# One double bank for the first transforms through the whole first half, full-row modal matmuls and later gating

## The chip, the core and the metric

The kernel runs on one core of a Trainium2 chip. TensorE (PE) multiplies matrices into PSUM, which has 8 banks of 128 x 512 words of 32 bits. VectorE (DVE), ScalarE (ACT) and GpSimd (POOL) do elementwise work, and DVE also transposes blocks of 32 x 32. SyncE (SP) issues nearly all transfers. Each engine works through its own instructions in order. The metric is the device time of one execution in microseconds (us), as the median of several.

## What is computed

Four layers are applied to one sequence of 2048 positions and 512 channels: A, B, A, B, each on a layer norm of x and added to x. Both layers are long causal convolutions per channel, done through Fourier transforms of length 4096.

```python
def _A_ref(q, k, v, shift_k, ssm_k, ssm_D):
    k_shift = 0
    for t in range(ks):
        k_shift = k_shift + k_pad[:, t:t + S, :] * shift_k[:, ks - 1 - t][None, None, :]
    kv = k_shift * v
    y = irfft(rfft(kv_pad) * rfft(kf_pad))[:S]
    y = y + kv * ssm_D[None, None, :]
    return q * y

def _B_ref(u, log_A_real, A_imag, C_real, C_imag, log_dt, D_skip):
    A = -jnp.exp(log_A_real) + 1j * A_imag
    C = (C_real + 1j * C_imag) * dt[:, None]
    P = jnp.exp((A * dt[:, None])[:, :, None] * pos[None, None, :])
    K = 2.0 * jnp.einsum("dn,dnl->dl", C, P).real
    y = irfft(rfft(u) * rfft(K))[:L]
    return y + u * D_skip[None, None, :]

x = x + _A_ref(_layernorm(x), ...)
x = x + _B_ref(_layernorm(x), ...)
x = x + _A_ref(_layernorm(x), ...)
x = x + _B_ref(_layernorm(x), ...)
```

The long convolution inside layer A does not depend on x (it works on `k` and `v` alone), so the kernel computes it once and uses it in both A layers. Layer B depends on x and is convolved twice. Its taps K, a sum over 128 modes for each channel and position, are computed once.

## The kernel before

**Transforms.** A forward transform has two matmul stages. The first stage (`fwd_group` and `fwd_rows`, line 171) multiplies a group of 32 channels by the table `wz`, once for each half `a` of the positions, into a tile `pf`. DVE then transposes `pf` into the tile z (lines 189 and 191; z is called `x`, `zk` or `zu` in the profile by whose it is). The second stage (`f2_chunk`, line 196) makes a tile `pu` with four matmuls. A transform of one quarter of the channels has 4 groups and then 8 chunks `pu`.

The first stage exists in two forms. Where the dictionary `psum` has a key `f1`, the group goes into one double bank (2 banks, 64 of the array's rows for each half, 512 columns). Where it has not, the table's rows of the other half are zero, all 128 rows are used, and the group takes two single banks under the tag `c1` (four matmuls of 256 columns). In the profile each matmul of 32-bit floats is two records, so a group is 4 records `64*128 64x512` in the first form and 8 records `128*128 128x256` in the second.

**Stages.** The first half of the program runs two streams of Python generators side by side, which a scheduler then merges and orders for each engine:

- `diagonal`, for layer A: the spectrum of `ssm_k` by quarters (`spectrum_quarter`, copies to `pc`, written to `spec`); the gating products kv of 16 groups (`gated`: four POOL products `term` on line 629, one ACT copy to a PSUM tile `acc`, three additions and a product `un` on DVE, written to `kv_d`); then `convolution`. A step of the convolution makes a chunk `pu`, multiplies it by the spectrum (ACT lines 281 and 282, DVE line 283, POOL lines 285 and 286, result `vv`), transforms back into `pi` (line 295, copied by ACT on line 296), and for each group through DVE (line 310) into `po` (line 316), which ACT copies to `ya`.
- `stream`, for layer B's taps: 64 steps, each with the angles `pa` (line 494, and line 499 after a rounding on DVE), the magnitudes `pm` (line 479), sines and exponentials on ACT, products `xye` on POOL and DVE, and a contraction into `pk` (line 531). Every four steps give 32 channels of taps, which go out to `kdram` and come back as `kk` for the spectrum of K (tile `zk`).

After both, `gated_update` adds layer A to x, row by row, the statistics and the norm follow, and the convolution of layer B begins.

**PSUM.** `pa` and `pm` share 3 banks and `pk` has one (pool `pp`). The other four banks are a stage pool, opened by `stage_banks`. Until the spectrum of `ssm_k` and the gating are through it holds two single banks `c1` and one double bank `f1`; before the convolution of layer A it is closed and opened again with four banks `c1` and none of the tag `f1`. Only after the first 16 steps of the first B convolution does a third pool take all 8 banks, 4 as `c1` and two double banks `f1`.

**Modal rows.** `load_rows` loads the modal parameters of 32 channels into `raw` (two kinds `k` on 128 partitions) and casts them to `rw`. Partitions 0 to 63 belong to steps 0 and 1 of the group and 64 to 127 to steps 2 and 3, so `mags` and `angles` multiply 64 rows at a time.

**Order.** The order of the code gives priorities. `run_steps` takes turns between one step of `stream` and two of `diagonal`. Before, one group of `gated` stands right behind the first step of the spectrum, and one third of a group (`next(kvs, 0)`) behind each of the 48 spectrum steps.

## Time and profile before

| | us |
|---|---|
| median of 3 runs | 742.3 |
| lowest and highest of them | 741.83, 750.0 |
| the profiled execution | 734.99 |
| span of its instructions | 733.2 |

The span is the time from the first to the last instruction of the profiled execution. It stands 1.8 us under that execution's own time, and 9.1 us under the median. Rows of the profile give a start and a duration in us; `x8` says that eight like instructions were merged into the row. A busy time counts a matmul from its start to the modelled end of its results, so that the share of a busy PE in which its array really streams is smaller.

By the profile, the first `pu` of layer A's convolution begins at 208.99 us and its last copy `ya` at 422.4 us. The update of x begins at 431.2 us, and the first `pu` of layer B's convolution at 480.64 us.

### The profile page before, as it was taken

What the parts mean: (1) busy time and instruction counts of PE and PEld (TensorE: products, weight loads), DVE (VectorE), ACT (ScalarE), POOL (GpSimd) and SP (SyncE); (2) the same over time, 40 slices, a digit from 0 to 9 for tenths busy, and PEclk for the clock granted to TensorE, in tenths of its full rate; (3) what the DMA queues carried; (4) which work ended last, traced back from release to release, by engine and by line L of the source; (5) the groups of instructions that cost most, each with busy time, mean ns of one, the idle gap of its engine ahead of it and who ended that gap; (6) DMA issues with size and microseconds to landing.
All of it is one profiled execution on the core that took longest, in us unless ns stands there. A gap on an engine that the chain in (4) does not pass through costs nothing. (4 is left out here: it accounts for less than half of the span.)

```text
span 733.2 us, 14282 instructions
## 1 busy us (share of the span) xinstructions
PE 593.9 (81%) x4984; PEld 409.9 (56%) x4984; DVE 531.1 (72%) x961; ACT 486.0 (66%) x882; POOL 454.8 (62%) x473
## 2 busy tenths in 40 slices
PE   1378877698989999969998865899798817799996
PEld 0154554456766776736765454767476503476773
DVE  7857959877385785584574877376597998978775
ACT  4246566577678777776798749677655447768672
POOL 5847969678268595684596620157576612479693
PEclk9997979768999999989999996999999978899999
DMA  9769767774745457636457493567866360178682
GB/s 324 258 227 315 255 209 235 226 249 158 223 125 143 130 127 204 167 107 173 118 149 212 136 335 150 170 181 203 226 192 164 85 172 0 51 209 238 195 244 100
DMA packets 80683, 135.39 MB, mean 185 GB/s; under 512 B 8540, under 2 KB 29412, under 8 KB 79460
## 3 DMA queue, kind: packets, MB, share of 16 engines
q1 hardware_dynamic: 79716, 132.06, 60.3%
q0 software_dynamic: 896, 2.43, 1.2%
q8 instruction: 39, 0.64, 0.4%
q14 instruction: 32, 0.26, 0.1%
HBM read 98.80 MB, written 35.65 MB: 183 GB/s over the span
## 5 line engine op out<-in xcount | busy, mean ns | idle before, releaser
L285 POOL TENSOR_TENSOR sw<-sw,kab 128x512 f32<-128x512 f32 x96 | 124.9, 1305 | 66.3 <-ACT sw L282 61.3
L283 DVE TENSOR_TENSOR vv<-pu,kab 128x512 f32<-128x512 f32 x96 | 65.1, 680 | 64.1 <-ACT sw L282 44.1
L295 PE MATMUL pi<-vv,mm 128*128 128x128 f32 x768 | 105.7, 281 | 6.7 <-DVE vv L283 4.3
L286 POOL TENSOR_TENSOR vv<-vv,sw 128x512 f32<-128x512 f32 x76 | 98.6, 1301 | 14.5 <-DVE vv L283 12.0
L295 PEld LDWEIGHTS pi<-vv,mm 128*128 128x128 f32 x768 | 94.2, 193 | 20.6 <-issue 10.4
L281 ACT ACTIVATE sw<-pu 64x512 f32<-64x512 f32 x96 | 57.1, 595 | 65.7 <-PE pu L196 61.8
L171 PE MATMUL pf<-kk,wz 128*128 128x256 f32 (+1 forms) x176 | 64.7, 624 | 42.1 <-issue 15.2
L517 POOL TENSOR_TENSOR xye<-co,m 128x512 f32<-128x512 f32 x64 | 76.0, 1187 | 36.5 <-ACT co L507 12.5
L629 POOL TENSOR_TENSOR term<-kvt 128x512 f32<-128x512 f32 x64 | 81.5, 1292 | 19.5 <-ACT acc L635 9.8
L196 PEld LDWEIGHTS pu<-zu,w 128*128 128x128 f32 x512 | 63.0, 191 | 42.8 <-DVE vv L283 16.1
L196 PE MATMUL pu<-x,w 128*128 128x128 f32 x512 | 79.6, 302 | 5.9 <-ACT pc L247 2.5
L196 PEld LDWEIGHTS pu<-x,w 128*128 128x128 f32 x512 | 70.7, 209 | 21.9 <-issue 7.5
L196 PE MATMUL pu<-zu,w 128*128 128x128 f32 x512 | 72.8, 284 | 10.7 <-DVE vv L283 9.6
L171 PE MATMUL pf<-u,wz 128*128 128x256 f32 (+2 forms) x280 | 76.4, 485 | 3.0 <-DVE zu L189 1.2
L247 ACT COPY pc<-pu 128x512 f32<-128x512 f32 x64 | 37.2, 587 | 45.3 <-PE pu L196 22.6
L485 ACT ACTIVATE m<-pm 128x512 f32<-128x512 f32 x96 | 53.4, 607 | 18.5 <-PE pm L479 15.1
L316 PE MATMUL po<-w,w 128*64 128x512 f32 x192 | 53.9, 637 | 13.8 <-DVE w L310 12.0
L171 PEld LDWEIGHTS pf<-kk,wz 128*128 128x128 f32 (+1 forms) x176 | 30.1, 222 | 58.2 <-issue 29.3
L505 ACT ACTIVATE co<-pa 128x512 f32<-128x512 f32 x64 | 38.4, 600 | 30.2 <-PE pa L499 29.8
L282 ACT COPY sw<-pu 64x512 f32<-64x512 f32 x96 | 55.5, 578 | 1.1
L518 DVE TENSOR_TENSOR xye<-pa,m 128x512 f32<-128x512 f32 x64 | 43.7, 683 | 13.8 <-ACT pa L506 7.3
L479 PE MATMUL pm<-tg,rw 64*128 64x512 f32 x96 | 43.7, 517 | 10.5 <-DVE xye L519 8.3
(137 smaller groups left out, 1147.3 us busy)
## 6 DMA issues: line engine op xcount, KB each, us to landing
kab<-spec SPq DMA_DIRECT2D x188, 256.0 KB, 4.3
spec<-pc SPq DMA_DIRECT2D x64, 256.0 KB, 2.3
kvt<-kv_in SPq DMA_DIRECT2D x16, 624.0 KB, 5.3
yaq<-ya_d SPq DMA_DIRECT2D x5, 1024.0 KB, 7.5
kk<-ssmk_in SPq DMA_DIRECT2D x16, 256.0 KB, 5.1
kv_d<-un SPq DMA_DIRECT2D x16, 256.0 KB, 4.1
xt<-x_in SPq DMA_DIRECT2D x16, 256.0 KB, 2.9
kdram<-ks SPq DMA_DIRECT2D x64, 64.0 KB, 2.9
```

The lines of the kernel that those rows point to most:

```text
L171: yield T.matmul(o, w, rhs, start=True, stop=True)
L196: ins = T.matmul(pu[:, i, :], w2[:, c * CK + i, :], z[:, :, c * CK + i, :], start=True, stop=True)
L281: S.mul(sw[0:64], pu[64:128], -1.0)
L282: swapped[0] = S.copy(sw[64:128], pu[0:64])
L283: V.tensor_mul(vv, pu, kabs[s][:, 0])
L285: (V if last else G).tensor_mul(sw, sw, kabs[s][:, 1])
L286: (V if last or s % add_dve == add_dve - 1 else G).tensor_add(vv, vv, sw)
L295: i1s[t] = T.matmul(pi[:, i, :], mm[:, c * CK + i, :], vvs[t][:, i, :], start=True, stop=True)
L316: ins = T.matmul(po[64 * a:64 * a + 64], w4, ws[g][:, :, 16 * a:16 * a + 16, :].rearrange("p x t r -> p t x r"), start=True, stop=True, ti ...
L485: i = S.activation(m, pm.rearrange("p (c i) -> p c i", c=16 if col == 2 else 8), AF.Exp)
L517: G.tensor_mul(xye[:, 0, :, 32:96], co[:, :, 1:65], m[:, :, 32:96])
L629: G.tensor_mul(term, kvt[:, 3 - j:19 - j, :], tap(j))
```

## The change

Five edits go together.

1. The second call `stage_banks(4, 0)` is gone. The stage pool keeps two banks `c1` and the double bank `f1` through layer A's convolution, so that all first stages of the first half take the pair form.
2. The stage pool and the pool of `pa` and `pk` are closed, and the pool of 4 banks `c1` and two double banks is opened, before `gated_update` rather than after the first 16 steps of the B convolution.
3. `raw` and `rw` get one more dimension, h: for each half the 64 other partitions are zero. `mags` and `angles` multiply all 128 rows. Two fixed tiles `raw` are zeroed once, and the tensor `rows_d` becomes one.
4. No group of `gated` stands in front any more (KV0 = 0), and the thirds of groups begin behind the fourth spectrum step (KS = 3).
5. The prologue of layer A's convolution (7 steps of `main`) is merged with the gating that is left over.

```diff
     def load_rows(gi):
-        raw = wk.tile([128, 2, 128], F32, name="raw", tag="raw", bufs=2)
+        raw = raws[gi % 2]
         q, g = divmod(gi, 4)
-        for k in range(2):
-            nc.sync.dma_start(raw[:, k, :], rows_d[k][q, :, g, :])
-        rows[gi] = wk.tile([128, 2, 128], F32R, name="rw", tag="rw", bufs=2)
+        for h in range(2):
+            hs = slice(64 * h, 64 * h + 64)
+            nc.sync.dma_start(raw[hs, h], rows_d[:, q, hs, g, :].rearrange("k p n -> p k n"))
+        rows[gi] = wk.tile([128, 2, 2, 128], F32R, name="rw", tag="rw", bufs=2)
         V.tensor_copy(rows[gi], raw)
...
-        rhs = tabs["tg2"][hs] if col == 2 else tabs["tg1"][hs, 8 * s:8 * s + 8, :]
-        mt = T.matmul(pm, rows[gi][hs, 1, :], rhs, start=True, stop=True)
+        rhs = tabs["tg2"] if col == 2 else tabs["tg1"][:, 8 * s:8 * s + 8, :]
+        T.matmul(pm, rows[gi][:, h, 1, :], rhs, start=True, stop=True)
...
-        T.matmul(pa, rows[gi][hs, 0, :], tabs["tt"][hs, 8 * s:8 * s + 8, :], start=True, stop=False,
+        T.matmul(pa, rows[gi][:, h, 0, :], tabs["tt"][:, 8 * s:8 * s + 8, :], start=True, stop=False,
...
-        KV0 = 1
+        KV0 = 0
+        KS = 3
...
-                    if q == 0 and i == 1:
-                        for grp in range(KV0):
-                            for _ in gated(grp):
-                                pass
...
-                    next(kvs, 0)
+                    if 12 * q + i >= KS:
+                        next(kvs, 0)
...
+            main = convolution(0, {"conv": ap}, steps_a, finish_a, lag=LAGA, ahead=AHA, nk=NKA, ns=NSA, nw=NWA, inplace=True,
+                               add_dve=ADA, zlast=zlast)
+            for _ in range(NCH - 1):
+                next(kvs, 0)
+                next(main)
+                yield
             for _ in kvs:
                 yield
-            stage_banks(4, 0)
-            yield from convolution(0, {"conv": ap}, steps_a, finish_a, lag=LAGA, ahead=AHA, nk=NKA, ns=NSA, nw=NWA, inplace=True,
-                                   add_dve=ADA, zlast=zlast)
+            yield from main
...
+    sctx.close()
+    pctx.close()
+    pp2 = ctx.enter_context(tc.tile_pool(name="ps2", bufs=1, space=PSUM, reuse_waits="tile"))
+    psum["c1"] = (pp2, 4)
+    psum["f1"] = (pp2, 2)
     with ExitStack() as yctx:
         yp = sbuf(yctx, "yp", "right")
...
     gctx.close()
-    sctx.close()
-    pctx.close()
-    pp2 = ctx.enter_context(tc.tile_pool(name="ps2", bufs=1, space=PSUM, reuse_waits="tile"))
-    psum["c1"] = (pp2, 4)
-    psum["f1"] = (pp2, 2)
     pools["conv"] = sbuf(ctx, "conv_b")
```

Three places of the merged order follow. Rows give the line, the operation, the tiles (output, then inputs) and the shape of the access. Lines from 460 on move by a few in the changed kernel: 472 becomes 479, 479 becomes 485, 494 becomes 499, 499 becomes 504, 531 becomes 536.

The first place is DVE at the start of the program, behind the last preparation of the modal parameters. Here `x<-pf` transposes a group of the `ssm_k` spectrum, `acc` and `un` belong to the gating, and `rw` is the cast of the modal rows with which the 64 tap steps begin. Before:

```order
L189 STREAM_TRANSPOSE x<-pf 128x512 x2
L637 TENSOR_TENSOR acc<-acc,term 128x512 x5
L639 TENSOR_TENSOR un<-acc,kvt 128x512
L637 TENSOR_TENSOR acc<-acc,term 128x512
L189 STREAM_TRANSPOSE x<-pf 128x512 x2
L639 TENSOR_TENSOR un<-acc,kvt 128x512
L189 STREAM_TRANSPOSE x<-pf 128x512 x2
L637 TENSOR_TENSOR acc<-acc,term 128x512
L472 CAST rw<-raw 128x256 x2
```

And now:

```order
L189 STREAM_TRANSPOSE x<-pf 128x512 x6
L479 CAST rw<-raw_234 128x512
L479 CAST rw<-raw_237 128x512
L642 TENSOR_TENSOR acc<-acc,term 128x512 x3
L644 TENSOR_TENSOR un<-acc,kvt 128x512
```

Nine gating instructions that stood ahead of the casts stand behind them now, and the casts have twice the columns.

The second place is PE in layer A's convolution, early in its run. Before, with single banks and full rows for `pf`, and half rows for `pa<-tt,rw`:

```order
L295 MATMUL pi<-vv,mm 128x128 x4
L171 MATMUL pf<-u,wz 128x16x8x2 x4
L499 MATMUL pa<-y,minus 128x512
L494 MATMUL pa<-tt,rw 128x512 x2
L171 MATMUL pf<-kk,wz 128x16x8x2 x4
L531 MATMUL pk<-xye_231 32x64 x16
L196 MATMUL pu<-x,w_104 128x128 x4
```

And now:

```order
L171 MATMUL pf<-u,wz 128x16x16x2 x2
L196 MATMUL pu<-x,w_103 128x128 x4
L295 MATMUL pi<-vv,mm 128x128 x3
L536 MATMUL pk<-xye_232 32x64 x16
L485 MATMUL pm<-tg_202,rw 128x512 x2
L295 MATMUL pi<-vv,mm 128x128
L171 MATMUL pf<-u,wz 128x16x16x2 x2
```

A group of the first stage is two matmuls here where it was four, on 64 rows where it was on 128; `pu`, `pi` and `po` now take turns on two banks.

The third place is PE at the end of layer A's convolution, from its last `po` on. Before:

```order
L316 MATMUL po<-w,w_106 64x512 x2
L171 MATMUL pf<-kk,wz 128x16x8x2 x8
L531 MATMUL pk<-xye_231 32x64 x16
L531 MATMUL pk<-xye_233 32x64 x16
L171 MATMUL pf<-kk,wz 128x16x8x2 x4
L196 MATMUL pu<-zk,w_104 128x128 x32
L171 MATMUL pf<-kk,wz 128x16x8x2 x16
L196 MATMUL pu<-zk,w_104 128x128 x32
L171 MATMUL pf<-u,wz 128x16x8x2 x16
L196 MATMUL pu<-zu,w_104 128x128 x4
```

And now:

```order
L295 MATMUL pi<-vv,mm 128x128 x12
L316 MATMUL po<-w,w_105 64x512 x8
L196 MATMUL pu<-zk,w_103 128x128 x32
L171 MATMUL pf<-kk,wz 128x16x16x2 x8
L196 MATMUL pu<-zk,w_103 128x128 x32
L171 MATMUL pf<-u,wz 128x16x16x2 x10
L196 MATMUL pu<-zu,w_103 128x128 x12
```

The last two contractions `pk` and three of the seven groups `pf<-kk` that stood behind the last `po` now stand ahead of it, and five groups of layer B's first stage, not four, stand ahead of its first `pu`. Over the whole program, up to the last `pu<-zk`, PE changes 132 times between 64-row and full 128 x 128 matmuls before and 72 times now.

More of the change, by code (lines that the diff above doesn't have):

```diff
@@ L118 @@
     kv_d = [dram.tile([128, 512], F32, name=f"kv_d{g}") for g in range(16)]
-    rows_d = [dram.tile([NQ, 128, 4, 128], F32, name=f"rows_d{k}") for k in range(2)]
+    rows_d = dram.tile([2, NQ, 128, 4, 128], F32, name="rows_d")
     cpool = sbuf(ctx, "cpool")
@@ L457 @@
         factors.append(xye)
+    raws = []
+    for i in range(2):
+        raw = wk.tile([128, 2, 2, 128], F32, name=f"raw{i}")
+        for h in range(2):
+            G.memset(raw[64 - 64 * h:128 - 64 * h, h], 0.0)
+        raws.append(raw)
     rows, ms, pks, angs = {}, {}, {}, {}
@@ L491, in angles @@
         h, s = divmod(k, 2)
-        hs = slice(64 * h, 64 * h + 64)
         pa = pp.tile([128, 512], F32, name="pa", tag="pa", bufs=NPA)
-        T.matmul(pa, rows[gi][hs, 0, :], tabs["tt"][hs, 8 * s:8 * s + 8, :], start=True, stop=False,
+        T.matmul(pa, rows[gi][:, h, 0, :], tabs["tt"][:, 8 * s:8 * s + 8, :], start=True, stop=False,
                  skip_group_check=True)
```

2 lines of the change are left out of this document (1 added, 1 removed).

## The prediction

> **What bounds the kernel now.** I read the busy times by stage first, then the chain of waits where the two layers meet, then single matmuls in the timeline. Stretches of the span, with the busy time of each engine (number of instructions in brackets), the granted TensorE clock, and the DMA share:
>
> ```profile
> span 733.2 us, 14282 instructions
> core 0: us, PE busy (x) PEld busy (x) DVE busy (x) ACT busy (x) POOL busy (x), PEclk, DMA share, GB/s
> 39.00:209.00 170.00, 142.48 (x1288) 92.85 (x1288) 123.97 (x229) 106.94 (x187) 113.88 (x123) 0.86 0.70 228
> 209.00:423.00 214.00, 193.37 (x2120) 137.63 (x2121) 142.72 (x229) 169.31 (x293) 152.06 (x155) 0.98 0.55 150
> 423.00:481.00 58.00, 39.92 (x277) 33.87 (x276) 35.81 (x86) 40.53 (x89) 7.51 (x16) 0.88 0.66 221
> ```
>
> In the 214 us in which layer A's convolution runs beside the taps, PE is busy 90%, ACT 79%, POOL 71%, DVE 67%. PE is the first limit there and ACT the next. In the 170 us before, PE has 84% and DVE 73%. From 423 to 481 us no engine is full, so a chain of waits sets the time. The chain that ended last shows it (start, us, what):
>
> ```profile
> 423.45 3.63 DMA kk<-kdram
> 428.17 6.91 DMA yaq<-ya_d
> 435.15 7.51 DMA yaq<-ya_d
> 455.90 2.66 DMA kk<-kdram
> 465.39 3.57 DMA spec<-pc
> 472.39 1.99 PE pf L171 x8
> 474.38 5.46 PE pf L171 x24
> 480.64 1.16 PE pu L196 x8
> ```
>
> So the last quarter of the taps (kk) and the update of x (yaq) are woven together there, and layer B's first stage (4 groups, 32 records of pf from 472.39) comes behind both.
>
> **The start (edit 4).** POOL, DVE and PE in the timeline (start, us):
>
> ```profile
> 26.74 8.71 POOL L629 TENSOR_TENSOR term<-kvt 128x512 f32<-128x512 f32 x7 [2.29 <-ACT acc L635]
> 28.13 3.16 DVE L637 TENSOR_TENSOR acc<-acc,term 128x512 f32<-128x512 f32 x5
> 35.41 0.24 POOL L239 TENSOR_TENSOR kk<-kk,dr 1x32 f32<-1x32 f32 x1
> 39.19 3.78 PE L196 MATMUL pu<-x,w 128*128 128x128 f32 x16 [1.41 <-DVE x L189]
> 43.26 2.07 DVE L472 CAST rw<-raw 128x256 fp32r<-128x256 f32 x2
> ```
>
> The fourth group of the spectrum waits at 35.41 for the small POOL addition kk, which stands behind seven products term (8.71 us). By the order now only four products stand ahead of it, so up to 3 x 1.24 = 3.7 us go, and DVE has nine gating instructions (9 x 0.63 = 5.7 us by the row of five) out of the way of the casts rw. The first pu and the first tap step should come 4 to 6 us earlier. The gating is only moved: the three groups that come later (12 POOL products of 1.24 us) fall into stretches in which POOL is 67 to 71% busy, and they are wanted only when their channels are transformed, so I cost them at nothing; without that cover they would cost at most 12 x 1.24 = 15 us of POOL. I take -5 us, between 0 and -6. The casts get twice the columns: at 2.07 / 2 = 1.04 us each, 16 casts that double would add at most 17 us of DVE over the whole first half; DVE is not the limit, so nothing is added.
>
> **Pairs of 64 rows instead of full rows (edits 1 and 2).** PE in the timeline, first full-row work in a row, then pairs between full-row work:
>
> ```profile
> 248.90 1.05 PE L196 MATMUL pu<-x,w 128*128 128x128 f32 x8
> 249.79 1.05 PE L295 MATMUL pi<-vv,mm 128*128 128x128 f32 x8
> 205.09 1.99 PE L171 MATMUL pf<-u,wz 128*128 128x256 f32 x8
> 206.74 0.82 PE L499 MATMUL pa<-y,minus 128*128 128x512 f32 x2
> 481.73 1.13 PE L171 MATMUL pf<-u,wz 64*128 64x512 f32 x4
> 482.79 2.05 PE L196 MATMUL pu<-zu,w 128*128 128x128 f32 x16
> 484.77 1.13 PE L171 MATMUL pf<-u,wz 64*128 64x512 f32 x4
> 485.83 1.16 PE L196 MATMUL pu<-zu,w 128*128 128x128 f32 x8
> ```
>
> A full group keeps PE 206.74 - 205.09 = 1.65 us. A group as pairs keeps it 485.83 - 484.77 = 1.06 us. Eight full records take 249.79 - 248.90 = 0.89 us where no 64-row work is near, but the sixteen from 482.79 take 1.98, not 1.78: 0.20 us for the change of form. So a group saves 1.65 - 1.26 = 0.39 us alone and up to 0.59 where pairs stand together; I take 0.5. Of 32 groups that change form, 16 (layer A) and 5 (zk) lie in the full 214 us: 21 x 0.5 = 10.5 us of PE. The other 7 of zk and 4 of layer B lie in the chain after 423 us; there PE is busy 69% and waits for transfers and copies, so of at most 11 x 0.5 = 5.5 us I count 1 us.
>
> **Full rows for the modal matmuls (edit 3).** In the timeline a half-row pa, its full-row partner and the next half-row one, and then a full-row one before a pu:
>
> ```profile
> 203.82 0.49 PE L494 MATMUL pa<-tt,rw 64*128 64x512 f32 x1
> 204.24 0.49 PE L499 MATMUL pa<-y,minus 128*128 128x512 f32 x1
> 204.67 0.49 PE L494 MATMUL pa<-tt,rw 64*128 64x512 f32 x1
> 258.49 0.71 PE L499 MATMUL pa<-y,minus 128*128 128x512 f32 x2
> 259.03 1.05 PE L196 MATMUL pu<-x,w 128*128 128x128 f32 x8
> ```
>
> With a change of form each takes 0.42 us; without one, two take 259.03 - 258.49 = 0.54 us. A half-row stretch and the way back thus cost 0.85 - 0.54 = 0.31 us. The order counts 132 changes between 64 rows and the full array before and 72 now; the 48 groups of pairs bring nearly all of the 72 and are already priced with theirs, those of before some 30 of the 132. About 100 changes, 50 round trips, go: 50 x 0.31 = 15 us of PE, of which 37 of the 64 tap steps, so 9 us, lie in the full 214 us and 6 in the 170 us before. There PE has slack, and I count half, -3 us. Two half-row matmuls on different halves could have run side by side before; that loss is inside the 0.31, since it was taken from neighbours that don't.
>
> **What the two missing banks cost (edit 1).** One pu in the timeline:
>
> ```profile
> 208.99 2.28 PE L196 MATMUL pu<-x,w 128*128 128x128 f32 x18
> 211.12 0.59 ACT L281 ACTIVATE sw<-pu 64x512 f32<-64x512 f32 x1
> 211.73 0.58 ACT L282 COPY sw<-pu 64x512 f32<-64x512 f32 x1
> 212.34 0.69 DVE L283 TENSOR_TENSOR vv<-pu,kab 128x512 f32<-128x512 f32 x1 [1.63 <-ACT sw L282]
> ```
>
> From its first matmul to the end of vv a bank is held 213.03 - 208.99 = 4.0 us. A pi, po or chunk of zk has one ACT copy of 0.58 us instead of the three readers, so about 2.2 us with its matmuls. The stage has 32 pu, 32 pi, 16 po and 16 chunks of zk: 32 x 4.0 + 64 x 2.2 = 269 us of bank time. Over four banks that is 67 us each and no matter; over two it is 134 us of about 200, so a bank is often still held when PE comes to it. The trace has this very layout, two banks c1 and a double bank, in the 170 us before, where 32 pu and 16 acc use them. Who waited for whom there (total, times, longest):
>
> ```profile
> PEld pu L196 <- ACT pc L247: 4.2, 5, 1.3
> PEld pu L196 <- DVE un L639: 3.7, 5, 1.3
> PE pu L196 <- ACT pc L247: 2.9, 5, 1.1
> ```
>
> That is 7.9 us for 48 uses, 0.16 us a use; 96 uses give 16 us. I take +16. The lower end is half of it (8 us), if the order suits the banks better; the upper end is one ACT instruction of 0.59 us at every use, 57 us. The Trainium skill, TensorEngine Tiling (Array Packing), Gotcha 1 (PSUM Pressure), speaks against the change here: row tiling puts more pressure on PSUM, as different row tiles write to different banks and may not use one at the same time. This case agrees in that a pair takes a double bank out of the four; the page gives no price.
>
> **The end of the stage (edit 2 and the order).** SP issued the second pair of yaq loads late, behind a small load dr that waited for the trip of kk through DRAM (423.45 + 3.63 us, then the yaq of 428.17). The taps now end ahead of the last po, so that wait, about 2 us of the chain, goes. With the 1 us of pairs I count -3 us. The pools' new place costs nothing by itself: the new double banks lie where pa, pm and pk were, which are free by then, and the last chunks of zk only hold the banks that layer B's pu take after them, as before.
>
> **The sum.** Start -5, early stage -3, full stage -10.5 - 9 + 16 = -3.5, end -3: -14.5 us. The profiled execution took 734.99 us and would take about 720.5. The median of the runs is 742.3, 7.3 us over that execution, so the forecast for the median is 742.3 - 14.5 = 728 us, a change of -2.0%, at the edge of what a measurement of this kernel can tell from no change, which I take as 2%, or 14.8 us (727.5).
>
> **The rivals.**
>
> Two banks become the bound. Each of the 96 uses then waits about one ACT instruction, 0.59 us: +57 instead of +16, so 742.3 - 14.5 + 41 = 769 us. For it speaks that ACT is 79% busy and DVE waits for ACT's sw before vv, so a bank comes free late; against it that pu, pi and tap work alternate, and the nearest stretch shows 0.16 us. The change stops paying at (16 + 14.5) / 96 = 0.32 us a use and is slower by 2% from 0.47 us. Chance 0.12.
>
> The banks are covered. PE has the tap matmuls to do while a bank drains; then the 16 us are at most 4, and the time is about 742.3 - 14.5 - 12 = 716 us. For it: taps and layer A are independent, the order was made with two banks in view, and the taps have their own banks. Against it: PE takes its work strictly in order. Chance 0.33.
>
> PE's relief lies beside ACT. If ACT's 169 us with their waits hold the stage, the saved PE time is idle time, and only the start and the end pay: 742.3 - 8 = 734 us. ACT's 79% speaks for it, PE's 90% against. Chance 0.15.
>
> The clock falls. The granted clock is 0.98 where PE is busy 90% and 0.86 where it is 84%. If relief and bank waits bring the full stage to 84%, its PE time of some 170 us grows by 0.12 of itself, 20 us: 748 us. The Trainium skill, TensorE: Matmul & The Clock Gate, Part 1, has the clock drop only after idle windows of about 3.4 us; by that rule waits near 1 us would leave it alone, and the time stays 728. The waits for banks shown above are at most 1.3 us. Chance 0.05.
>
> **How the numbers follow.** The forecast (about 728, both sides of the 2% line) has 0.35, and the rivals 0.33, 0.15, 0.05 and 0.12. Faster by over 2%: the covered banks, 0.33, and somewhat under a third of the forecast's own 0.35, together 0.43. Slower by over 2%: the bound by banks, 0.12. Within 2%: the rest, 0.45. The likeliest case alone reaches from 720 (bank waits of 8 us) to 736. The range leaves out the slower half of the first rival and the far end of the second, where nearly all gains add up: 709 to 750.
>
> **What would show it.** Right: first pu of the spectrum near 35 us and the first cast rw near 35 us; no 64-row records of pm and pa; 4 records of about 0.65 us for every group of pf up to layer A's end; first pu of layer A's convolution some 8 us earlier; waits of PE for ACT sw, ie, pc and DVE vv summing to 10 to 25 us in layer A's convolution, which lasts 205 to 215 us; kk's trip gone from the chain behind the last ya. Wrong: those waits above 45 us, a granted clock under 0.9 in that stage, or a PE that is less busy while the stage keeps its 214 us.

## The result and the profile after

| | before | after |
|---|---|---|
| median of 4 runs each | 742.07 us | 757.12 us |
| lowest and highest | 741.48, 750.0 | 756.28, 766.31 |
| the profiled execution | 734.99 | 766.31 |

The measured ratio is 1.0324, with a 95% interval from 1.0269 to 1.0379. The eight times of the table alone give less, 757.12 / 742.07 = 1.020 by medians; which further times of before the ratio goes by is not known. So the change costs 2 to 3%, 15 to 24 us. The forecast was 728 us with a range of 709 to 750, so sign and range were both missed. The profiled execution of after is the slowest of its four, that of before lies 7 us under its median and under all four: the two traces differ by 31 us, the medians by 15. Differences of less than about 10 us between two traces are therefore not read here unless a second pair of kernels shows them too. Runs of the kernel before on the chips of the experiments lay between 727.95 and 751.32 us, so each experiment is compared with the runs of before on its own chip. In the table of the experiments the ratios leave out runs in a slower state and the medians do not, so the two can differ by about 1% (e15: 737.12 against 741.36 us by medians, ratio 1.0055).

First the same two stretches as were shown of before (busy time of PE, PEld, DVE, ACT and POOL with the number of instructions, then clock, DMA share, GB/s), and the stretch from the first pu of layer A's convolution to its last ya, which the trace of after puts at 221.61 and 449.82 us:

```profile
39.00:209.00 170.00, 135.10 (x1210) 83.61 (x1209) 129.81 (x223) 96.78 (x168) 119.07 (x124) 0.80 0.66 214
209.00:423.00 214.00, 184.29 (x2028) 122.61 (x2026) 144.87 (x237) 170.09 (x296) 150.60 (x157) 0.94 0.55 153
...
222.00:450.00 228.00, 194.08 (x2121) 126.80 (x2121) 146.15 (x234) 167.69 (x292) 155.60 (x159) 0.91 0.53 149
```

Against before, DVE and POOL are busier from 39 to 209 us (129.81 and 119.07 against 123.97 and 113.88 us) while PE is less busy. Layer A's convolution takes 228 us instead of 214. PE's busy time in it did not fall (194.08 against 193.37 us): it has less to stream, but at a clock of 0.91 instead of 0.98, and it idles 34 us instead of 21.

The start, in the timeline of after (start, us, what):

```profile
32.31 3.78 PE L196 MATMUL pu<-x,w 128*128 128x128 f32 x16 [1.41 <-DVE x L189]
35.11 0.67 POOL L464 MEMSET raw<- 64x256 f32 x2 [5.43 <-DMA rows_d<-hl]
38.23 0.43 DVE L479 CAST rw<-raw 128x512 fp32r<-128x512 f32 x1 [5.98 <-DMA raw<-rows_d]
39.48 0.43 DVE L479 CAST rw<-raw 128x512 fp32r<-128x512 f32 x1 [0.82 <-DMA raw<-rows_d]
```

The first pu comes 6.9 us earlier than before (39.19) and the first cast 5.0 us earlier (43.26). Yet the first pu of layer A's convolution comes 12.6 us later (221.61 against 208.99). So the stretch between lost some 18 us and the convolution 14 us.

The forms of the matmuls, in the groups of after up to 510 us (operation, shapes, count, busy us, mean ns, idle us before them and what ended it):

```profile
L485 PE MATMUL pm<-tg,rw 128*128 128x512 f32 x96 | 43.5, 518 | 4.3 <-ACT m L491 3.4 <-DVE rw L479 0.7 <-DVE xye L524 0.2
L499 PE MATMUL pa<-tt,rw 128*128 128x512 f32 x64 | 29.7, 485 | 7.1 <-DVE xye L524 6.1 <-ACT m L491 0.9
L171 PE MATMUL pf<-u,wz 64*128 64x512 f32 x84 | 25.3, 684 | 3.8 <-issue 1.4 <-DVE x L189 1.3 <-DVE zu L189 1.0
```

The change does what it says: pm and pa have all 128 rows, and pf from u stands in pairs of 64 rows only. What PE waited for in after from 222 to 450 us (total, times, longest):

```profile
PE po L316 <- DVE w L310: 7.6, 7, 2.0
PE pu L196 <- ACT x L296: 4.8, 6, 1.3
PE pk L536 <- DVE ks L546: 4.6, 2, 4.3
...
PE pi L295 <- ACT x L296: 2.0, 3, 1.0
PE po L316 <- ACT x L296: 1.6, 2, 0.8
...
PE pu L196 <- DVE vv L283: 1.2, 3, 0.6
```

Waits of pu, pi and po for the ACT copy x of another chunk are waits for a bank. In before the same view, from 209 to 423 us, has one of 0.6 us. Here those quoted, with vv, make 4.8 + 2.0 + 1.6 + 1.2 = 9.6 us. The row pk behind DVE's ks has one wait of 4.3 us; what lies behind it is the main finding below.

The end, in the timeline of after:

```profile
449.23 0.59 ACT L682 COPY ya<-po 128x512 f32<-128x512 f32 x1 [2.82 <-PE po L316]
...
452.08 1.64 SPq L730 DMA_DIRECT2D yaq<-ya_d  x2
...
458.43 1.95 ACT L741 ACTIVATE ut<-yaq,rs 128x512 f32<-128x512 f32 x3 [3.61 <-DMA yaq<-ya_d]
```

From the last ya to the first use of yaq it takes 458.43 - 449.82 = 8.6 us, before 431.2 - 423.0 = 8.2 us. The trip of kk comes behind that, as before:

```profile
461.48 14.40 SPq L248 DMA_DIRECT2D spec<-pc  x5
...
475.97 2.27 SPq L229 DMA_DIRECT2D kk<-kdram  x2
...
478.77 0.24 POOL L239 TENSOR_TENSOR kk<-kk,dr 1x32 f32<-1x32 f32 x1 [44.91 <-DMA kk<-kdram]
...
490.95 6.81 PE L196 MATMUL pu<-zk,w 128*128 128x128 f32 x40 [1.51 <-DVE zk L189]
```

The last taps were done at 429.1 us, but SP issues the last two loads of kk at 475.97, behind five writes of the spectrum (461.48 + 14.40). The spectrum of K waits for them, and layer B's first stage comes behind it. From the last ya to the first pu of layer B (508.3) it takes 58.5 us, before 57.7.

### The profile page after: what moved, and what is told of

Its sections match the earlier page's. It is cut to its first block, busy times and chain, and to the rows that moved or that the text cites. A ratio compares the mean times of both kernels' runs of the same rounds, so it can differ in the third digit from the quotient of the medians.

```text
span 764.5 us, 14021 instructions
## 1 busy us (share of the span) xinstructions
PE 596.0 (78%) x4856; PEld 390.3 (51%) x4856; DVE 535.0 (70%) x961; ACT 485.9 (64%) x882; POOL 455.9 (60%) x477
## 5 line engine op out<-in xcount | busy, mean ns | idle before, releaser
L196 PE MATMUL pu<-x,w 128*128 128x128 f32 x512 | 82.3, 309 | 15.6 <-ACT pc L247 6.9
L196 PEld LDWEIGHTS pu<-x,w 128*128 128x128 f32 x512 | 74.1, 216 | 37.5 <-ACT pc L247 8.9
L171 PE MATMUL pf<-kk,wz 64*128 64x512 f32 x128 | 58.4, 857 | 38.4 <-DMA kk<-ssmk_in 12.6
L196 PE MATMUL pu<-zu,w 128*128 128x128 f32 x512 | 72.7, 285 | 11.2 <-DVE vv L283 10.9
L316 PE MATMUL po<-w,w 128*64 128x512 f32 x192 | 59.8, 712 | 15.4 <-DVE w L310 12.2
L171 PE MATMUL pf<-u,wz 64*128 64x512 f32 (+2 forms) x200 | 61.4, 647 | 5.6 <-DVE zu L189 2.2
L536 PE MATMUL pk<-xye 128*32 128x64 f32 x2048 | 54.3, 244 | 11.2 <-POOL xye L526 6.5
L196 PE MATMUL pu<-zk,w 128*128 128x128 f32 x256 | 42.2, 319 | 22.4 <-ACT pc L247 17.8
L536 PEld LDWEIGHTS pk<-xye 128*32 128x32 f32 x2048 | 39.1, 122 | 39.7 <-issue 20.9
L523 DVE TENSOR_TENSOR xye<-pa,m 128x512 f32<-128x512 f32 x64 | 43.4, 678 | 20.1 <-ACT pa L511 10.9
```

The source lines that it names most:

```text
L171: yield T.matmul(o, w, rhs, start=True, stop=True)
L196: ins = T.matmul(pu[:, i, :], w2[:, c * CK + i, :], z[:, :, c * CK + i, :], start=True, stop=True)
L316: ins = T.matmul(po[64 * a:64 * a + 64], w4, ws[g][:, :, 16 * a:16 * a + 16, :].rearrange("p x t r -> p t x r"), start=True, stop=True, ti ...
L536: T.matmul(pk[32 * i4:32 * i4 + 32, 2 * k + i, :], xye[:, r, 4 * i + i4, 64:96], xye[:, r, 4 * i + i4, 0:64], start=r == 0, stop=r == 1, t ...
```

## The experiments

Each kernel is the kernel before with the edit named, or the changed kernel with a part undone. The edits have the numbers of the section on the change. The table has the median beside that of before on the same chip, the ratio with its interval, and from the trace the first pu of layer A's convolution, its length to the last ya, and the span. For e4 and e8 only the times are given.

| kernel | what it is | median, before (us) | ratio | first pu | length | span |
|---|---|---|---|---|---|---|
| before | | 742.07 | 1 | 209.0 | 214.0 | 733.2 |
| after | edits 1 to 5 | 757.12, 742.07 | 1.0324 [1.0269, 1.0379] | 221.6 | 228.2 | 764.5 |
| e1 | edit 3 | 736.84, 735.75 | 1.006 [1.0013, 1.0106] | 221.1 | 203.2 | 733.6 |
| e2 | edit 4 | 754.70, 735.75 | 1.0288 [1.0216, 1.0361] | 232.9 | 206.9 | 748.1 |
| e3 | edits 1, 2 | 751.78, 735.75 | 1.0256 [1.0193, 1.0320] | 207.8 | 236.8 | 752.1 |
| e4 | edits 2, 3, 4 | 745.97, 735.75 | 1.014 [1.0037, 1.0243] | | | |
| e5 | edits 1, 2, 3, 5 | 753.58, 739.09 | 1.0226 [1.0132, 1.0319] | 209.6 | 230.2 | 749.0 |
| e7 | two single banks | 774.65, 739.09 | 1.0515 [1.0420, 1.0610] | 219.1 | 235.9 | 768.3 |
| e8 | e3, pairs twice | 778.87, 739.09 | 1.0552 [1.0466, 1.0637] | | | |
| e9 | e2, pu twice | 748.42, 739.09 | 1.0165 [1.0067, 1.0264] | 232.5 | 201.3 | 743.3 |
| e10 | three single banks | 750.40, 743.45 | 1.0118 [1.0055, 1.0181] | 212.1 | 221.5 | 748.4 |
| e11 | KV0 = 2 | 753.62, 743.45 | 1.0155 [1.009, 1.022] | 219.9 | 218.3 | 747.6 |
| e12 | edit 3, no casts | 722.73, 743.45 | 0.9731 [0.9687, 0.9774] | 212.7 | 200.9 | 721.8 |
| e13 | edits 2, 3, no casts | 720.76, 743.45 | 0.9685 [0.9634, 0.9736] | 211.4 | 201.0 | 721.5 |
| e14 | no casts | 733.25, 741.36 | 0.9876 [0.9847, 0.9904] | 214.1 | 212.3 | 734.3 |
| e15 | edits 1 to 5, no casts | 737.12, 741.36 | 1.0055 [1.0004, 1.0105] | 211.8 | 210.4 | 732.1 |
| e16 | edit 4, no casts | 733.40, 741.36 | 0.9851 [0.9808, 0.9893] | 225.5 | 198.1 | 733.0 |
| e17 | edit 4, casts unread | 755.64, 738.65 | 1.0316 [1.0217, 1.0414] | 233.7 | 211.2 | 755.8 |
| e18 | edits 2, 3, 4, no casts | 724.93, 738.65 | 0.9854 [0.9793, 0.9916] | 219.4 | 190.9 | 721.3 |
| e19 | edits 1, 2, no casts | 744.43, 738.65 | 1.0131 [0.9998, 1.0265] | 204.5 | 230.1 | 740.4 |

The scheduler puts out another order for each edit, so the first pu moves by some us where the edit has no business there (e7 and e10, whose code differs from before only from the convolution on). The length has to be read with the first pu beside it: layer A's convolution shares its time with the taps, and a kernel that begins it late has fewer of the 64 tap steps in it, as more of them stand ahead of it or behind it. By the products xye on DVE, 38 steps lie in the convolution of before, 35 in that of e1, 40 in e14, 33 in e12 and 32 in e16. So the last ya (first pu plus length) and the span say more than the length alone.

### One part alone: e1, e2, e3

e1 is edit 3 without the others:

```diff
-        T.matmul(pa, rows[gi][hs, 0, :], tabs["tt"][hs, 8 * s:8 * s + 8, :], start=True, stop=False,
+        T.matmul(pa, rows[gi][:, h, 0, :], tabs["tt"][:, 8 * s:8 * s + 8, :], start=True, stop=False,
...
```

> The kernel before with edit 3 alone (full rows for pm and pa). Layout of the banks and the gating are as before. If the loss comes from the banks or from the gating, this is the same as before or up to 1.5% faster (50 round trips of 0.31 us saved): 731 to 743 us. If the loss comes from the full rows themselves (the longer casts rw on DVE, which took 26.3 us in the changed kernel against 17.4, or a granted clock that falls as PE has less to do), this is slower: 750 to 757 us, with a clock under 0.90.

The time is the same within 2% (0.6% longer): the convolution is 11 us shorter and the stretch before it 12 us longer. That is not yet the gain that was forecast (-9), since there is less to do in the later stretch: PE has 1981 records in it, and 2120 in the convolution of before.

```profile
221.00:424.00 203.00, 181.45 (x1981) 135.78 (x1982) 134.02 (x216) 161.48 (x280) 147.18 (x148) 0.97 0.56 154
```

What full rows are worth is seen only without the casts, in e12 and e14 below.

e2 is edit 4 alone:

```diff
-        KV0 = 1
+        KV0 = 0
+        KS = 3
...
```

> The kernel before with edit 4 alone (no gated group in front, the thirds from the fourth spectrum step on). If the late gating is what lengthened the stretch up to the last pu of the ssm_k spectrum (185 us before, 202 us after), this shows a last spectrum pu at 195 us or later and a time of 750 us or more. If the banks or the full rows are the cause, the start is some 5 us earlier and the time 737 to 743 us.

It costs 2.9%, though its first pu of the spectrum comes at 34.6 us; the last one comes at 200 us (195 or later was expected of the late gating). The first pu of the convolution is 24 us late. The step "I cost them at nothing" is wrong in this kernel.

e3 is edits 1 and 2 (without 5):

```diff
             for _ in kvs:
                 yield
-            stage_banks(4, 0)
...
```

> The kernel before with edits 1 and 2 alone (double bank and two single banks through layer A's convolution, the last pool opened early; no merging of the prologue). If two banks are the cause: 755 to 765 us, with the convolution of layer A longer than the 214 us from its first pu to its last ya, and waits of PE for ACT and DVE readers of pu, pi and pc of over 20 us in it. If they are not: 733 to 743 us.

It costs 2.6%, somewhat less than expected (751.78 us, not 755 to 765). The loss is all in the convolution, 237 us instead of 214. But PE's waits for ACT and DVE readers in it, which were expected above 20 us, sum to about 5 us (pu for x 2.1 and for vv 1.6, pi for ya 0.7 and for vv 0.4). PE is busy for 208.6 us there instead of 193.4, at a lower clock.

### One part undone: e4, e5

e4 is the changed kernel with four single banks in the convolution again (edits 1 and 5 undone), e5 the changed kernel with the old gating (edit 4 undone):

```diff
...
             for _ in kvs:
                 yield
+            stage_banks(4, 0)
...
```

> The changed kernel with edits 1 and 5 undone: four single banks again for layer A's convolution, which starts behind all gating. If two banks cost the time, this is 740 us or less, since it keeps the full rows. If the stretch before the convolution cost it (gating, full rows), it stays at 750 to 757 us.

```diff
-        KV0 = 0
-        KS = 3
+        KV0 = 1
...
```

> The changed kernel with edit 4 undone (one gated group in front and the thirds from the first step on; pairs, early pool, full rows and the merged prologue stay). Edit 4 alone made the kernel before 2.9% slower, with its first pu of layer A's convolution 24 us later. If the gating costs the same inside the changed kernel, this is 10 to 20 us faster than the changed kernel, 2% or less over the kernel before, with that first pu at 210 us or earlier. If the merged prologue hides the gating, it stays 2.5 to 3.5% over the kernel before.

By the ratios each undoing takes back a part of the 3.2%: 1.8% with four banks, 1.0% with the old gating (the intervals reach some 1% to each side). By medians it is 5 us and 0.6 us of the 15, so that the second part isn't shown. e4 falls between the two outcomes that were expected, and e5 gains less than its 10 to 20 us, though with the old gating the first pu of the convolution is back at 209.6 us. No single edit is the whole loss, and the three lone losses of e1 to e3 (0.6 + 2.9 + 2.6 = 6.1%) are more than that of all together, which suggests that the edits share a cause.

### Banks or the clock: e7, e8, e10

e7 gives layer A's convolution of the kernel before two single banks, with its full rows for pf, and e10 three:

```diff
-            stage_banks(4, 0)
+            stage_banks(2, 0)
```

> The kernel before with two single banks instead of four in layer A's convolution, no double bank and no pairs there. Theory banks: what lengthened that stage from 214 to 237 us with pairs alone is the lack of two banks, so it is as long or longer here, 235 us or more, and the whole 2.5% or more over the kernel before, whatever the clock does. Rival clock: pairs leave PE with less to do, the granted clock falls (0.89 in that stage with pairs, 0.98 before), and the stage stretches by it; then full rows on two banks keep 0.95 or more and the stage is under 225 us.

```diff
-            stage_banks(4, 0)
+            stage_banks(3, 0)
```

> The kernel before with three single banks in layer A's convolution in place of four; all else is unchanged. Theory (too few banks cost the time): the stage from the first pu of layer A's convolution to the last ya lasts between the four banks' 203 to 214 us and the two banks' 236 us, and nearer to four, about 218 us, as a use waits only when all other banks are held; ratio 1.00 to 1.02. Rival (two banks lost for another reason, for instance an order of the work that was written for four): the stage is as long as with two, 230 us or more, ratio above 1.03.

e8 is e3 with each matmul of a pair issued twice in the convolution, so that PE is busier in the same two banks:

```diff
+            if twice[0] and not full:
+                T.matmul(o, w, rhs, start=True, stop=True)
             yield T.matmul(o, w, rhs, start=True, stop=True)
...
```

> The kernel with pairs alone (edits 1 and 2), and each matmul of a pair issued twice while layer A's convolution is recorded; the first result is overwritten by the same one. It adds some 1 us of PE for each of about 28 groups. Theory banks: PE gets more work on top of its waits, and the stage stays at 237 us or grows, up to 20 us more. Rival clock: the granted clock rises towards 0.98 and the stage is shorter than 237 us in spite of the added work.

The convolution of e3, of e7 and of e10, as stretches:

```profile
208.00:445.00 237.00, 208.60 (x2131) 134.16 (x2131) 152.15 (x241) 174.83 (x302) 156.11 (x162) 0.87 0.51 141
```

```profile
219.00:455.00 236.00, 203.24 (x2047) 140.75 (x2046) 132.15 (x218) 164.21 (x283) 146.71 (x148) 0.93 0.49 136
```

```profile
212.00:434.00 222.00, 201.59 (x2151) 141.33 (x2151) 138.75 (x227) 165.70 (x288) 152.21 (x154) 0.97 0.53 144
```

With four, three and two single banks the stage lasts 214, 222 and 236 us, without a single pair in it: the number of banks alone stretches it. It isn't the casts either (the next but one section): in e7 and e10 they take 12.6 and 10.9 us, less than the 17.4 of before. The clock is 0.87 in e3 and 0.93 in e7 and the length is the same, so the length doesn't follow the clock alone. e8, with more for PE to do, was not faster than e3 but slower, by ratios 1.0552 against 1.0256, and its clock in the stage, 0.87 from 215 to 473 us of an execution 1.7% above its median, had not risen. How the missing banks make the stage longer is less clear than that they do: e7 idles 33 us where before idles 21, with 13 us of waits for readers of a bank, but in e3 PE idles only 28 us and is busy longer. How much of that the lower clock adds isn't settled, since every kernel with fewer banks also has the lower clock.

### The clock before the convolution, and the gating's place: e9, e11

In e2 the granted clock from 39 to 209 us is 0.73, before 0.86. e9 is e2 with each pu matmul of the ssm_k spectrum issued twice:

```diff
-            ins = T.matmul(pu[:, i, :], w2[:, c * CK + i, :], z[:, :, c * CK + i, :], start=True, stop=True)
+            for _ in range(times):
+                ins = T.matmul(pu[:, i, :], w2[:, c * CK + i, :], z[:, :, c * CK + i, :], start=True, stop=True)
...
```

> The kernel with edit 4 alone, and each second-stage matmul pu of the ssm_k spectrum issued twice (the same result overwritten): 32 x 0.9 = 29 us more PE work before layer A's convolution, where the clock was 0.73 against 0.86. Rival clock: the clock there rises above 0.8 and the first pu of the convolution comes no later than 233 us. Theory load (POOL, DVE and the shared banks hold the gating back, and the clock only follows): the clock rises little and that pu comes later than 233 us, up to 29 us.

The clock rises to 0.87 and the first pu of the convolution comes at 232.5 us, as the rival had it. The ratio is 1.0165 against 1.0288, with intervals that overlap. That alone could not tell whether the clock or another order helped; e16 below could. e11 goes the other way and puts two groups in front:

```diff
-        KV0 = 1
+        KV0 = 2
```

> The kernel before with two groups of gating in front of the first spectrum steps in place of one (KV0 = 2), the contrary of edit 4. Theory (gating that is done before 60 us, where POOL and DVE have room, is taken out of a full stretch): the first pu of the spectrum comes 4 to 6 us later than 39.2 us, the last term before 174 us, and the first pu of layer A's convolution no later than 212 us; ratio 0.99 to 1.01. Rival (the front delays everything behind it by its own length): the first pu of layer A's convolution at 214 us or later, ratio above 1.01.

The last term ends at 174.1 us and the first pu of the spectrum at 41.2, yet the first pu of the convolution comes 11 us later than before: the rival's times, and 1.6% slower. More in front loses too, so "gating belongs into the idle stretch" is no explanation either. The casts that the next section is about take 25.7 us in e11, against 17.4 in before.

### What takes it back: the casts rw on DVE (e12, e13, e14 to e17)

The prediction costed the casts at nothing. The group of them in before, in e2 and in after, over the whole span (busy us, mean ns):

```profile
L472 DVE CAST rw<-raw 128x256 fp32r<-128x256 f32 x16 | 17.4, 1090 | 0.0
```

```profile
L472 DVE CAST rw<-raw 128x256 fp32r<-128x256 f32 x16 | 21.9, 1366 | 3.5 <-DMA raw<-rows_d 3.5
```

```profile
L479 DVE CAST rw<-raw 128x512 fp32r<-128x512 f32 x16 | 26.3, 1645 | 6.8 <-DMA raw<-rows_d 6.8
```

The shortest cast of 256 columns takes 0.28 us in before and e2, the shortest of 512 columns 0.39 us in after. So most of these sums is standing still. One place in the timeline of after shows beside what:

```profile
274.00 1.05 PE L295 MATMUL pi<-vv,mm 128*128 128x128 f32 x8
...
275.32 2.53 POOL L285 TENSOR_TENSOR sw<-sw,kab 128x512 f32<-128x512 f32 x2
...
275.94 5.20 DVE L479 CAST rw<-raw 128x512 fp32r<-128x512 f32 x1
...
277.44 1.16 PE L196 MATMUL pu<-x,w 128*128 128x128 f32 x8 [0.87 <-ACT x L296]
277.80 1.19 POOL L522 TENSOR_TENSOR xye<-co,m 128x512 f32<-128x512 f32 x1
278.94 0.69 POOL L526 TENSOR_TENSOR xye<-co,m 128x256 f32<-128x256 f32 x1
279.59 1.26 POOL L286 TENSOR_TENSOR vv<-vv,sw 128x512 f32<-128x512 f32 x1
281.06 0.68 DVE L283 TENSOR_TENSOR vv<-pu,kab 128x512 f32<-128x512 f32 x1
281.66 0.60 DVE L545 TENSOR_TENSOR ks<-pk,dt 128x256 f32<-128x256 f32 x1
282.10 0.63 DVE L546 TENSOR_TENSOR ks<-pk,dt 128x256 f32<-128x256 f32 x1
...
282.87 0.44 PE L536 MATMUL pk<-xye 128*32 128x64 f32 x8 [4.27 <-DVE ks L546]
```

A cast that needs 0.4 us stands for 5.2 us, as long as POOL has one instruction behind the other; it ends at 281.14, when POOL's vv (279.59 + 1.26 = 280.85) is done. Behind it DVE's vv and ks wait, and PE, which wants the one bank pk, idles from 278.60 to 282.87: that is the wait of 4.3 us in the table of waits. From 39 to 450 us of after the casts take between 0.39 and 6.75 us, while each other large group of DVE keeps to its time: xye with 512 columns 0.65 to 0.71, vv 0.65 to 0.69, w, a transpose from SBUF to SBUF, 1.22 to 1.25.

The other casts show the same. Thirteen of the traces have casts, 208 in all. Of these, 158 take longer than 0.31 us (256 columns) or 0.44 us (512 columns), and every one of the 158 ends 0.15 us (256) or 0.28 to 0.29 us (512) after the end of a POOL instruction. So it is POOL's instructions that let a cast go. No cast stood past a gap between two POOL instructions. Where one follows directly upon the other, 102 times the cast got through and 147 times it did not; what decides that isn't shown.

The Trainium skill, SBUF — State Buffer, section "SBUF: two separate sides", says that DVE and GpSimd share a port pair as an exclusive lock, which DVE needs for two-port modes, and that a 32-bit tensor_copy from SBUF to SBUF starts such a mode. The trace agrees, with 5.20 us for 0.4. By the page the winner has the pair for the whole instruction; here a cast stood beside five in a row. That what POOL holds is this port pair no run here shows.

e12 is e1 without the casts. The rows are rounded already when they are written to DRAM, so they can be loaded straight into a tile of the type that the matmuls read:

```diff
-        raw = wk.tile([128, 2, 2, 128], F32, name=f"raw{i}")
+        raw = wk.tile([128, 2, 2, 128], F32R, name=f"raw{i}")
...
-            nc.sync.dma_start(raw[hs, h], rows_d[:, q, hs, g, :].rearrange("k p n -> p k n"))
-        rows[gi] = wk.tile([128, 2, 2, 128], F32R, name="rw", tag="rw", bufs=2)
-        V.tensor_copy(rows[gi], raw)
+            nc.sync.dma_start(raw[hs, h].bitcast(F32), rows_d[:, q, hs, g, :].rearrange("k p n -> p k n"))
+        rows[gi] = raw
...
```

> The kernel before with full rows for the modal matmuls (edit 3), the rows loaded straight into the tile that the matmuls read, so that DVE casts nothing. Theory (edit 3 gains about 10 us in layer A's convolution and loses as much before it because the longer casts hold DVE): the convolution lasts 203 to 207 us, its first pu comes at 205 to 212 us, ratio 0.985 to 0.995. Rival (the early loss is a matter of the merged order, not of the casts): the first pu comes at 218 us or later as with edit 3 alone (221.1 us), ratio 1.00 to 1.01.

722.73 us, 2.7% faster than before, which is more than the theory gave. The first pu comes 8 us earlier than in e1. The 16 casts of e1 had summed to 20.6 us. From 39 us to the last ya, the two stretches of e12:

```profile
39.00:209.00 170.00, 137.30 (x1378) 90.22 (x1378) 121.12 (x227) 111.59 (x195) 120.24 (x133) 0.91 0.70 227
213.00:414.00 201.00, 181.19 (x1915) 135.61 (x1914) 123.55 (x201) 158.57 (x274) 142.69 (x144) 0.97 0.58 158
```

In the first one PE gets through 1378 records, in e1 through 1257: without the casts more is done by then.

e13 adds edit 2 (its diff stands in the section on the change, the pools' new place):

> The same full rows without casts, with the 8-bank pool opened before the update of x (edit 2) and four single banks in layer A's convolution. Theory (edit 2 alone brings nothing, since the chain from the last ya to the first pu of layer B is one of transfers): from the last ya to the first pu of layer B stays at 57 to 60 us, and the ratio is that of the kernel without edit 2 within 0.5%. Rival (early pairs of layer B's first stage and of the last taps shorten that chain): 54 us or less, and the ratio 0.5% or more below.

From the last ya to the first pu of layer B it takes 57.7 us, in e12 60.1, and the spans are 721.5 and 721.8 us. Edit 2 alone brings nothing that can be measured.

e14, e15 and e16 take the casts out of the kernel before, of the changed kernel and of e2, in the same way:

```diff
-        raw = wk.tile([128, 2, 128], F32, name="raw", tag="raw", bufs=2)
+        raw = wk.tile([128, 2, 128], F32R, name="raw", tag="raw", bufs=2)
...
-        V.tensor_copy(rows[gi], raw)
+        rows[gi] = raw
```

> The kernel before with half rows as they were, the modal rows loaded straight into the tile that the matmuls read, so that DVE casts nothing. Theory (the casts hold up DVE and so the taps; full rows add their own gain in layer A's convolution): ratio about 0.985, with the convolution of layer A at 210 to 214 us and its first pu 2 to 5 us earlier than 209 us. Rival (the gain belongs to the casts alone): ratio 0.97 to 0.975 as with full rows and no casts. Second rival (the casts are hidden and full rows gain all): ratio 1.00.

> The changed kernel, all five edits, with the modal rows loaded without casts. Theory (two banks too few and the later gating cost their price independently of the casts): ratio 1.00 to 1.01, layer A's convolution still 225 us or longer, its first pu at 212 to 218 us. Rival (the casts carried the loss of the later gating): first pu at 208 us or earlier, ratio 0.99 or below.

> The kernel before with the later gating (edit 4) and no casts, half rows. Theory (the later gating itself costs, since POOL, DVE and ACT are taken from the taps and the spectrum in a full stretch and the clock falls): against the kernel without casts and with the old gating it loses 1.5% or more, the first pu of layer A's convolution comes at 220 us or later, and the granted clock between 39 and 209 us stays under 0.82. Rival (the casts behind POOL carried that loss): within 1% of the kernel without casts and with the old gating, first pu at 215 us or earlier.

All three ran on one chip: 733.25, 737.12 and 733.40 us, with 741.36 for before. The ratio of e14, 0.9876, is the one that the theory gave, but its first pu comes 5 us later than in before and not 2 to 5 us earlier, and the runs of before on that chip reach from 729.49 to 746.56 us, those of e14 from 732.20 to 736.09. So what the casts cost the kernel before, 0 to 9 us, is not clear of the scatter.

Against e14, e12 has the full rows beside. Its last ya comes at 413.6 us and that of e14 at 426.4: 12.8 us for full rows, 10.5 by medians on two chips. The convolution of e14:

```profile
214.00:426.00 212.00, 197.34 (x2120) 139.54 (x2121) 136.15 (x225) 172.26 (x299) 151.96 (x155) 0.97 0.55 152
```

Without casts the later gating costs nothing (733.40 against 733.25), where with them it cost 19 us. The stretch from 39 to 209 us of e2, and then of e16:

```profile
39.00:209.00 170.00, 133.99 (x1138) 84.81 (x1138) 122.00 (x214) 94.88 (x167) 119.05 (x124) 0.73 0.63 206
```

```profile
39.00:209.00 170.00, 140.04 (x1206) 90.98 (x1205) 118.57 (x214) 100.50 (x177) 121.37 (x126) 0.76 0.66 217
```

Its clock is 0.76, hardly above the 0.73 of e2, and the first pu of its convolution is as late as 225.5 us; yet the time is that of e14, since the convolution, with 32 tap steps in it and not 40, then takes 198 us. So neither the low clock nor the late start was the loss: of e16's expectation the rival's time came true, but not the early first pu that it gave. e15 is 20 us faster than after by medians on two chips; its ratio is within what the theory gave, but its convolution takes 210 us where 225 or more was expected. So much of the changed kernel's long stage was the casts, though the profiled execution of after overstates it.

e17 decides how. It is e16 with the 16 casts made into a tile that nothing reads:

```diff
+        rw = wk.tile([128, 2, 128], F32R, name="rw", tag="rw", bufs=2)
+        V.tensor_copy(rw, raw.bitcast(F32))
         rows[gi] = raw
...
```

> The kernel before with the later gating (edit 4); the modal rows are loaded straight into the tile that the matmuls read, and DVE still makes the 16 casts, into a tile that nothing reads. Theory (a cast stands still beside a busy POOL and holds up DVE's queue, whoever reads it): as slow as with real casts, ratio 1.02 to 1.03. Rival (the loss was the path from the transfer over the cast to the modal matmuls): as fast as without casts, ratio 0.98 to 0.99. Between the two: both carry a part.

It is as slow as e2, 1.0316. Its casts:

```profile
L472 DVE CAST rw<-raw 128x256 fp32r<-128x256 f32 x16 | 26.5, 1656 | 8.8 <-DMA raw<-rows_d 8.8
```

Nobody waits for these casts, so the cost is DVE's queue that they hold up. 26.5 us of casts, 16 x 0.28 = 4.5 of it work, cost 755.8 - 733.0 = 22.8 us of span against e16, about one us for each us that DVE stands still. That is no fixed price: the casts of e2 take only 4.5 us more than those of before, and e2 is 19 us slower. So it matters where in the program a cast stands, and which places are the dear ones stays open. That POOL is the one a cast stands behind is read from the ends of the 158 casts above, not from a kernel in which POOL alone was changed.

### What gained together, and the banks again: e18, e19

e18 joins edits 2, 3 and 4 without casts and with four banks; e19 is e3 without casts. Both combine diffs that stand above.

> Full rows, the early 8-bank pool and the later gating (edits 2, 3 and 4), four single banks in layer A's convolution, no casts. Theory (the later gating costs nothing without casts, and full rows gain about 1.5%): ratio 0.96 to 0.975. Rival (with full rows the later gating still loses): ratio above 0.98. Against the changed kernel without casts it also gives the price of edits 1 and 5: at least 2.5% if the two missing banks cost about 30 us.

> Edits 1 and 2 (the double bank kept, two single banks in layer A's convolution) without casts, half rows. Theory (two banks are too few by themselves): against the kernel without casts and with four banks, 0.9876, it loses 2 to 3%, ratio 1.005 to 1.02, the convolution of layer A lasts 228 us or longer. Rival (the casts that hold DVE are what keeps two banks full): ratio 1.00 or below, the convolution lasts 222 us or less.

The span of e18 is 721.3 us, as that of e13 is 721.5, but its ratio is 0.9854 against 0.9685, on another chip. The ratio speaks for the rival, the spans for the theory: what the later gating does beside full rows stays open within 1.7%. It is no gain. Against e15 it has four banks again and edit 5 undone, which is 12 us by medians, 1.7% and less than the 2.5% that was expected. e19 is 11 us slower than e14 by medians, its convolution takes 230.1 us instead of 212.3: two banks are too few by themselves, without any cast.

The fastest kernels are e13 and e12, 3.1 and 2.7% under before: full rows, four banks, the old gating, no casts.

## Why the prediction was wrong

**The start.** Right in size and place (-5 forecast; 5.0 and 6.9 us in the trace), but it did not count. e16 has its first pm more than 8 us ahead of e14 (36.3 against 44.9 us), and the same time.

**The moved gating, "I cost them at nothing".** Wrong in the kernel as it is: +19 us alone (e2). Of the cover that was named (POOL at 67 to 71%) POOL itself was not what gave out. The products term fill gaps of POOL, and a gap always let a waiting cast through. Without casts the step holds with half rows: 0.15 us between e16 and e14.

**The casts, "DVE is not the limit, so nothing is added".** This is the step of the prediction that failed most. It scaled a cast by its columns and put DVE's mean share beside it. The rows spoke against that already: 2.07 us for two casts of 256 columns, beside 0.68 us for operations of 512. What the runs show in its place: by medians against the same chip's before, casts cost 19 us in after (+15.05 with, -4.2 without: e15), 22 with full rows (e1 and e12, +1.1 and -20.7) and 25 with the later gating (e17 and e16); the ratios give 20, 24 and 34. In before it is 8 by medians (e14), which is not clear of the scatter. So after pays some 11 us more for them than before does by medians, and up to 20 by the ratios.

**Pairs and the two banks.** The relief of the pairs was put at 10.5 us and the banks at 16. Net of both, e19 against e14 loses 744.43 - 733.25 = 11 us by medians and 18 us in the convolution; e3 with casts 16 and 23. e15 against e18, with full rows, gives 12. Two banks without pairs (e7) cost 36, but there pf takes its banks from the same two. If the pairs bring their 10.5 (which no run here shows alone), the banks cost some 22 to 34 us, 0.23 to 0.35 a use. That is within the ends that were given, 8 to 57, but the value taken, 0.16, came from a stretch where 48 uses fell in 170 us, against 96 in 214 here. The first rival, two banks as the bound, had the right cause; but its 57 us and its 769 were too much, its waits were seen only in part (about 5 us in e3), and it was not alone.

**Full rows.** Right in sum: -9 in the convolution and -3 earlier were forecast, and e12 against e14 has its last ya 12.8 us earlier and a span 12.5 us shorter, 10.5 us by medians. How it divides between the two stretches the lengths don't tell.

**The end, -3 us.** Wrong. The taps did end ahead of the last ya (429.1 against 449.8 us), but that did not take the trip of kk out of the chain: SP issued its last loads at 475.97, behind writes of the spectrum. The first yaq was no earlier, 8.6 us behind the last ya against 8.2, and from there to layer B's first pu it took 58.5 us against 57.7.

**The clock.** The rival put it under 0.9 in the full stage; after has 0.91 there. It is lower in every kernel with fewer banks, but lengths don't follow it: 237 us at 0.87 (e3) and 236 at 0.93 (e7), and e16 at 0.76 before the convolution loses nothing.

**PE's relief beside ACT.** It does not hold for full rows: they gain some 10 us, beyond start and end, though ACT is as busy in e12's convolution (158.57 of 201 us, 79%) as in that of before.

**The sum.** Start -5, early -3, full rows -9, pairs and banks +5.5, end -3 made -14.5. Start and end bring nothing (8 us), pairs and banks cost some 11 instead of 5.5 (5.5 us), full rows are as forecast: that makes -1 us without the casts, where e15 against e14 on one chip measures +4. The 5 us between them are within the scatter. The casts' 11 us more make +4 into +15, the difference of the medians; the ratio of 1.0324 would ask for 24, and for 20 from the casts.

Of the signs that were named, the missing 64-row pm and pa, the pairs and the start came; kk's trip had not gone from the chain, and the convolution's first pu came 12.6 us late rather than 8 early. PE's waits for readers, at 9.6 us, were just under the low end of 10 to 25 while the stage took 228 us: the sign could not see a queue that is held up on DVE, which shows as a wait of pk for ks.

## What to carry to other kernels

Before an operation is costed at nothing because its engine is not full, compare the shortest and the mean duration of like operations: a mean of 1.09 us against 0.28 suggests that it waits for another engine while it holds its own queue, and work that is moved onto that other engine can make it longer. Keeping such an operation as work that nothing reads, beside a kernel without it, separates the held queue from the data path in two runs. Price a scarce buffer in the stage in which it will be scarce, by uses per us, and by one experiment with one buffer less.

## What was not expected of the hardware

A cast of 256 columns from SBUF to SBUF on DVE, 0.28 to 0.29 us beside an idle POOL in e2, stood up to 6.21 us in before and one of 512 columns up to 6.75 us in after, beside up to seven POOL instructions, and all that stood ended at a fixed distance, 0.15 or 0.28 to 0.29 us, behind the end of a POOL instruction. Full rows with these casts gained nothing (e1); without the casts, by loading the type that the matmuls read, they made the kernel 2.7% faster than before (e12).

The granted clock from 39 to 209 us was 0.91 in e12 and 0.76 in e16, and e16 was no slower than e14 at 0.80: PE did not set the time there.
